# Moving a statistics pool ahead of the weight tiles in a fused attention and two-layer kernel

## The chip, the cores and the metric

The kernel runs on one core of one Trainium2 chip. The metric is the device time of one execution in microseconds (us). Before the change three executions took 976.26, 979.25 and 979.58 us; the median is 979.25 us.

## The reference, cut to what matters

Attention with rotary positions (4 batches, 8 heads, 576 positions, head size 64) gives x of 2304 tokens by 512. Two feed-forward layers follow, both in float32:

```python
# layer 1, weights 512x1536, 512x1536, 1536x512
gate = 1.0 / (1.0 + np.exp(-(x @ w_gate)))
val = x @ w_val
y = gate * val @ w_out
# layer 2, weights 512x1024 and 1024x512
h = y @ w_in
sm = softmax(h)                       # over the 1024 columns
solu = h * sm
ln = (solu - mean(solu)) / np.sqrt(var(solu) + 1e-06) * g_ln
out = ln @ w_out2
```

The weights arrive as 64-bit floats and are decoded on the core.

## The kernel before, in words

Every product is made of three matmuls: both factors are split into a high part and a low part (float32r), and high by high, high by low and low by high are added in PSUM. Below, the *stationary* operand of a matmul is the one loaded into the array (128 columns, 512 bytes per partition), the *moving* one is streamed through it (512 columns are 2048 bytes per partition).

**Attention (to about 320 us of the span).** 16 pairs of heads are worked off in 144 groups. The order of the work is written out by hand in slots (SLOTS and the agenda). A pair's sums of weights go through `weigh_out` (L398): they are transposed, copied into the small tile `rt` (VectorE, L401) and stored by a DMA in SyncE's queue (L403), once per pair, about 17.5 us apart. The stacked operands of the scores are brought together by five DMAs from SBUF to SBUF (`stack`, L306 to L314).

**Layer 1 (about 303 to 760 us).** 60 items: three sets of four feature tiles, each over five token blocks of 512, 512, 512, 256 and 512 columns. An item is `gate_val` (24 matmuls, L672 to L674: stationary is the weight tile `w`, moving the split activations `xs`) and, one item later, `out_part` (12 matmuls, L781 to L783: stationary `w`, moving `gs`). Between them ScalarE, VectorE and GpSimd make `gs` (L762 to L767). While an item runs, `make` decodes the next weights in one to two units per item (`w_decode`: L119 to L136 on ScalarE, VectorE and GpSimd), and `split_x` splits the next activations (L504 to L507). Weight tile number i lies in ring slot i modulo 6: slot 0 is the pool `wA`, slots 1 to 5 are the pool `wB`.

**Layer 2 (about 760 us to the end).** Weight units lie in the same ring, tiles 12 to 17, three units each; units 0 to 2 are in slot 0 (`wA`). For each of 18 token tiles, `hidden` runs 24 matmuls (L874 to L876: stationary the split tokens `ysp`, moving the weight units 0 to 7, so the first nine of them read `wA` and the other fifteen `wB`), `normalise` makes the statistics in a small tile `st`, and `project` runs 24 matmuls (L969 to L971: stationary the transposed tokens `lt`, moving the weight units 8 to 15).

**Where tiles lie.** Pools opened on the left side follow one another in the order in which they are opened, tiles padded to 32 bytes per partition; pools on the right side are laid from the upper end. What matters below is each tile's start address modulo 512 bytes, worked out from that order and the tile sizes:

| tile | role | start modulo 512 |
|---|---|---|
| `w` in `wA` | stationary in layer 1, moving in layer 2 | 192 |
| `w` in `wB` | stationary in layer 1, moving in layer 2 | 288 |
| `xs`, `gs` (right side) | moving in layer 1 | 480 |
| `ysp` (tiles 0 to 3, in `xs` buffers) | stationary in layer 2 | 480 |
| `ysp` (tiles 4 to 17, left side) | stationary in layer 2 | 288 |
| `lt` (right side) | stationary in layer 2 | 480 |
| `ident`, `qtl` (before all) | attention | 128, 192 |
| `e`, alternating buffers | attention, stationary in transposes | 160, 416 |
| `et`, `vs` | attention, moving and stationary | 160, 160 |
| `st` of scores, by tile | attention, both | 288 and 32 |

All steps inside a tile (high to low part, one 128-row piece to the next) are whole multiples of 512 bytes for the tiles of both layers, so the table gives the residue of every matmul operand of the layers. The pool `s2` (three tiles `st` of 32 bytes) is opened after `wA` and `wraw`.

```python
    wA = ctx.enter_context(tc.tile_pool(name="wA", bufs=1))
    wraw = ctx.enter_context(tc.tile_pool(name="wraw", bufs=2))
    s2_p = ctx.enter_context(tc.tile_pool(name="s2", bufs=3))
```

Of the kernel before, what the change touches and what calls it, by code (L numbers as in the profile page):

```python
# [8 lines left out]
F32 = mybir.dt.float32  # L9
# [11 lines left out]
def kernel(  # L21
# [26 lines left out]
    P = 128  # L48
# [5 lines left out]
    NS = 3  # L54

    const = ctx.enter_context(tc.tile_pool(name="const", bufs=1))
    wA = ctx.enter_context(tc.tile_pool(name="wA", bufs=1))
    wraw = ctx.enter_context(tc.tile_pool(name="wraw", bufs=2))
    s2_p = ctx.enter_context(tc.tile_pool(name="s2", bufs=3))
    wdec = ctx.enter_context(tc.tile_pool(name="wdec", bufs=2))  # L60

    ident = const.tile([P, P], F32, name="ident")
# [112 lines left out]
    enter = a_ctx.enter_context  # L175
# [3 lines left out]
    rot_p = prep_ctx.enter_context(tc.tile_pool(name="rot", bufs=1, side="right"))  # L179
    qk_p = enter(tc.tile_pool(name="qkT", bufs=2))  # L180
    wt_p = enter(tc.tile_pool(name="wt", bufs=2))
    uw_p = enter(tc.tile_pool(name="uw", bufs=4))
    st_p = enter(tc.tile_pool(name="st", bufs=4))
    et_p = enter(tc.tile_pool(name="et", bufs=1))
# [158 lines left out]
    NTL = len(order)  # L343
# [53 lines left out]

    def weigh_out(i):  # L398
        ps = wts[i]
        rt = wt_p.tile([NTL, P], F32, tag="rt", name=f"rt{i}")  # L400
        nc.vector.tensor_copy(rt, ps[:NTL, :P])  # L401
        d = dr_p.tile([NTL * P], F32, tag="d", name=f"d{i}")
        nc.sync.dma_start(out=d.rearrange("(n p) -> n p", p=P), in_=rt)  # L403
        wts[i] = d
# [180 lines left out]
    for i in range(NPR):  # L585
# [14 lines left out]
        for name, fn in (  # L600
            ("weigh", weigh), ("weigh_t", weigh_t), ("weigh_out", weigh_out), ("spread", spread), ("scale", scale_x)
        ):
            at(g + own[name], REST, fn, i)
# [75 lines left out]
    if True:  # L679
# [32 lines left out]
        for g in range(NPR * NTL):  # L712
            i, n = divmod(g, NTL)
# [83 lines left out]
    def split_y(t):  # L797
        if t < 4:
            s = xs_pool["p"].tile([P, 2, 512], F32R, tag="xs", name=f"ysp{t}")
            s = s.rearrange("p a (k t) -> p a k t", k=KD)  # L800
        else:
            s = ys_p.tile([P, 2, KD, P], F32R, tag="ys", name=f"ysp{t}")
        src = y_sb[:, :, t * P:(t + 1) * P]
        nc.scalar.copy(out=s[:, 0], in_=src)
        nc.gpsimd.tensor_sub(out=s[:, 1], in0=src, in1=s[:, 0].bitcast(F32))
        ysp[t] = s
# [28 lines left out]
    for t, (s, bl, f) in enumerate(items):  # L835
# [17 lines left out]
        if f % FG in (1, 2) and t + FG < len(items):  # L853
            s2, bl2, _ = items[t + FG]
# [4 lines left out]
    enter = c_ctx.enter_context  # L859
# [6 lines left out]
    def hidden(t, half):  # L866
        s = ysp[t]
        if half == 0:
            phs[t] = ps_2.tile([P, 2, 512], F32, tag="s", name=f"ph{t}")
        ph = phs[t]  # L870
        for kk in range(2 * half, 2 * half + 2):
            for n in range(2):
                wh, wl = unit(2 * kk + n)
                nc.tensor.matmul(ph[:, n, :], s[:, 0, kk, :], wh, start=kk == 0, stop=False)  # L874
                nc.tensor.matmul(ph[:, n, :], s[:, 0, kk, :], wl, start=False, stop=False)  # L875
                nc.tensor.matmul(ph[:, n, :], s[:, 1, kk, :], wh, start=False, stop=kk == KD - 1)  # L876

    def spare(name):
        return xs_pool["p"].tile([P, 2, 512], F32R, tag="xs", name=name).rearrange("p n c -> p (n c)").bitcast(F32)

    def normalise(t):

        ph = phs.pop(t)
        st = s2_p.tile([P, 8], F32, tag="st", name=f"st{t}")
        nm, sm, tsum, var, r, rv = (st[:, j:j + 1] for j in range(6))
        yield nc.vector.tensor_reduce(out=nm, in_=ph, axis=AX.XY, op=ALU.max, negate=True)
        if t == 0:
            e = spare("e2_0")
        else:
            e = h_p.tile([P, DF2], F32, tag="e", name=f"e2_{t}")  # L890
        ev = e.rearrange("p (n c) -> p n c", n=2)
        yield nc.scalar.activation(out=ev, in_=ph, func=AF.Exp, bias=nm, accum_out=sm)
        yield nc.vector.scalar_tensor_tensor(
            out=ev, in0=ph, scalar=1.0, in1=ev, op0=ALU.mult, op1=ALU.mult, accum_out=tsum
        )

        nc.vector.tensor_scalar_mul(tsum, tsum, -1.0 / DF2)
        nc.vector.tensor_scalar_add(r, sm, 1e-9)
        nc.vector.reciprocal(r, r)
        if t == 0:  # L900
            junk = spare("junk0")
        else:
            junk = j_p.tile([P, DF2], F32, tag="junk", name=f"junk{t}")
        yield nc.scalar.activation(out=junk, in_=e, func=AF.Square, bias=tsum, accum_out=var)
        nc.vector.tensor_scalar(out=rv, in0=var, scalar1=r, scalar2=r, op0=ALU.mult, op1=ALU.mult)
        nc.vector.tensor_scalar(out=rv, in0=rv, scalar1=1.0 / DF2, scalar2=1e-6, op0=ALU.mult, op1=ALU.add)
        nc.gpsimd.tensor_tensor(out=rv, in0=rv, in1=mhalf, op=ALU.pow)
        yield
        nc.vector.tensor_mul(out=rv, in0=rv, in1=r)
        nc.vector.tensor_scalar(out=e, in0=e, scalar1=tsum, scalar2=rv, op0=ALU.add, op1=ALU.mult)  # L910
        ln[t] = e
        yield
# [6 lines left out]
    def pack(t):  # L919

        upper, lower = halves(ln.pop(t))
        pk = pk_p.tile([P, 2, DF2], U16, tag="pk", name=f"pk{t}")
        copy(PACK[0], pk[:, 0], upper)
        copy(PACK[1], pk[:, 1], lower)
        tps[t] = tp_p.tile([P, 2 * KF, P], U16, tag="tp", name=f"tp{t}")
        nc.sync.dma_start_transpose(out=tps[t], in_=pk.rearrange("p a c -> p (a c)"))

    def unpack(t):

        tp = tps.pop(t).rearrange("p (a k) t -> p a (k t)", a=2)  # L930
        z = z_p.tile([P, DF2], F32, tag="z", name=f"z{t}")
        upper, lower = halves(z)
        copy(UNPACK[0], upper, tp[:, 0])
        yield copy(UNPACK[1], lower, tp[:, 1])
        lt = lts[t] = lt_p.tile([P, 2, KF, P], F32R, tag="lt", name=f"lt{t}")
        z = z.rearrange("p (k t) -> p k t", k=KF)
        yield nc.scalar.copy(out=lt[:, 0], in_=z)
        yield nc.vector.tensor_sub(out=lt[:, 1], in0=z, in1=lt[:, 0].bitcast(F32))
# [23 lines left out]
    def project(t, half):  # L962
        lt = lts[t]
        if half == 0:
            pos[t] = ps_o.tile([P, DM], F32, tag="o", name=f"po{t}")
        po = pos[t]
        for f in range(KF // 2 * half, KF // 2 * half + KF // 2):
            wh, wl = unit(8 + f)
            nc.tensor.matmul(po, lt[:, 0, f, :], wh, start=f == 0, stop=False)  # L969
            nc.tensor.matmul(po, lt[:, 0, f, :], wl, start=False, stop=False)  # L970
            nc.tensor.matmul(po, lt[:, 1, f, :], wh, start=False, stop=f == KF - 1)  # L971
        if half == 0:
            return
        ob = o_p.tile([P, DM], F32, tag="ob", name=f"ob{t}")
        nc.scalar.copy(out=ob, in_=po)

        c = t * P
        while c < (t + 1) * P:
            b, j = divmod(c, S)
            if j < MAIN:  # L980
                r, p = divmod(j, P)
                n = min(P - p, (t + 1) * P - c)
                dst = out[b * S:b * S + MAIN, :].rearrange("(p r) d -> r p d", r=4)[r, p:p + n, :]
            else:
                n = min(S - j, (t + 1) * P - c)
                dst = out[b * S + j:b * S + j + n, :]
            nc.sync.dma_start(out=dst, in_=ob[c - t * P:c - t * P + n, :])
            c += n
# [20 lines left out]
    def do(kind, t):  # L1009
        if kind == "H":  # L1010
            hidden(t, 0)
            hidden(t, 1)
            norms[t] = normalise(t)
        elif kind == "n":
            next(norms[t])
        elif kind == "u":
            if t not in unpacks:
                unpacks[t] = unpack(t)
            next(unpacks[t])
        elif kind == "Y":  # L1020
            split_y(t)
        elif kind == "P":
            pack(t)
        elif kind == "J":
            project(t, 0)
            if t == NTT - 2:
                turn_ln(NTT - 1)
            project(t, 1)
        elif kind == "M":
            for _ in make_steps(1):  # L1030
                pass
        elif kind == "C":
            x = written.pop(0)
            next(x)
            next(x)
        elif kind == "O":
            out_part(*items[-1])
        elif kind == "S":
            store_y(*items[-1])
        elif kind == "X":  # L1040
            open_pools()
        elif kind == "T":

            st = s2_p.tile([P, 8], F32, tag="st", name="table_in")
            nc.scalar.activation(out=st[:, 0:1], in_=mhalf, func=AF.Exp)


# [68 lines left out]
```

## Time and profile before

| what | value |
|---|---|
| profiled execution, its own time | 976.1 us |
| its span | 974.1 us |
| work outside the span | 2.0 us |
| TensorE busy | 935.9 us (96%) |
| VectorE, ScalarE, GpSimd busy | 648.6, 500.6, 444.8 us |
| granted TensorE clock, mean | 0.992 |

PE is TensorE's matmuls, PEld its weight loads, DVE VectorE, ACT ScalarE, POOL GpSimd, SPq the queue of SyncE. The end of a matmul in the records is modelled: one matmul of 512 columns shows 0.39 us although the next one starts 0.23 us after it. So a pace is read from the starts of neighbouring matmuls and not from their durations.

### The profile page before, as it was taken

The numbers are of one execution on the slowest core, as the hardware profiler recorded it, in microseconds if no ns is written. First come the engines' busy times: TensorE is split into PE (matmuls) and PEld (weight loads), VectorE is DVE, ScalarE is ACT, GpSimd is POOL, SyncE is SP. The second block draws the span as 40 slices with busy tenths as digits, with TensorE's granted clock in tenths as the row PEclk, the third lists the DMA queues.
The fourth block names the chain that finished last, engine by engine and source line by source line (L and its number), as shares of the span: only waits on it lengthen the run. The fifth ranks groups of instructions, "written<-read, shape, count | busy, mean of one in ns | idle before, by whom it ended". The sixth has DMA issues, their size and how long they took to land.

```text
span 974.1 us, 14436 instructions
## 1 busy us (share of the span) xinstructions
PE 935.9 (96%) x5128; PEld 801.7 (82%) x5128; DVE 648.6 (67%) x1073; ACT 500.6 (51%) x994; POOL 444.8 (46%) x356
## 2 busy tenths in 40 slices
PE   4999999999999899999999999999999989999998
PEld 3899889898898688898788898788898868888886
DVE  8999889899988945346245355445456787666561
ACT  4888889798986422133111123112123576666662
POOL 5668888879846533334413344324343531121110
PEclk9999999999999999999999999999999999999999
DMA  4666676576654220103001012100112334234231
GB/s 109 143 170 165 161 178 171 140 196 158 159 144 136 87 65 22 43 23 108 22 22 44 23 44 87 44 22 22 44 45 64 109 65 87 66 77 86 65 76 43
DMA packets 92311, 86.10 MB, mean 88 GB/s; under 512 B 52608, under 2 KB 77456, under 8 KB 92240
## 3 DMA queue, kind: packets, MB, share of 16 engines
q1 hardware_dynamic: 92240, 85.19, 34.7%
q8 instruction: 40, 0.66, 0.3%
q14 instruction: 31, 0.25, 0.1%
HBM read 46.83 MB, written 4.79 MB: 53 GB/s over the span
## 4 chain that ended last, share of the span: by engine, by line
PE 64%; DVE 13%; DMA 10%; POOL 5%; issue 3%; ACT 3%; SPq 2%; DVEq 0%; POOLq 0%; ACTq 0%
DMA st<-st 9%; PE gv L673 9%; PE gv L674 9%; PE gv L672 9%; PE y L783 4%; PE y L781 4%; PE y L782 4%; PE po L970 3%; PE po L969 3%; PE po L971 3%; PE ph L874 3%; PE ph L875 3%; PE ph L876 3%; DVE nm L371 3%; PE av L476 2%
## 5 line engine op out<-in xcount | busy, mean ns | idle before, releaser
L767 POOL TENSOR_TENSOR gs<-g,gs 128x512 fp32r<-128x512 f32 (+1 forms) x59 | 74.0, 1254 | 268.3 <-DVE gs L766 242.2
L762 ACT ACTIVATE sg<-gv 128x512 f32<-128x512 f32 (+1 forms) x60 | 33.3, 555 | 297.0 <-PE gv L674 297.0
L672 PE MATMUL gv<-xs,w 128*128 128x512 f32 (+1 forms) x480 | 179.1, 373 | 1.6 <-ACT w L135 1.6
L674 PE MATMUL gv<-xs,w 128*128 128x512 f32 (+1 forms) x480 | 179.1, 373 | 1.1 <-POOL w L136 1.1
L673 PE MATMUL gv<-xs,w 128*128 128x512 f32 (+1 forms) x480 | 179.1, 373 | 0.3 <-DVE xs L507 0.2
L764 DVE TENSOR_TENSOR g<-gv,sg 128x512 f32<-128x512 f32 (+1 forms) x60 | 38.2, 636 | 181.5 <-ACT sg L762 181.4
L364 PE MATMUL s<-st 128*128 128x288 f32 x512 | 103.9, 322 | 14.9 <-DMA st<-st 8.3
L376 ACT ACTIVATE e<-s,nm 128x576 f32<-128x576 f32 x144 | 107.3, 745 | 17.6 <-DVE nm L371 17.1
L371 DVE TENSOR_REDUCE nm<-s 128x1 f32<-128x576 f32 x144 | 107.2, 745 | 6.3 <-PE s L364 4.8
L672 PEld LDWEIGHTS gv<-xs,w 128*128 128x128 f32 x480 | 90.4, 188 | 19.4 <-ACT w L135 2.1
L674 PEld LDWEIGHTS gv<-xs,w 128*128 128x128 f32 x480 | 90.4, 188 | 19.3 <-POOL w L136 1.9
L673 PEld LDWEIGHTS gv<-xs,w 128*128 128x128 f32 x480 | 90.5, 189 | 19.1 <-DVE xs L507 1.9
L429 DVE TENSOR_TENSOR et<-te,et 128x512 fp32r<-128x512 f32 x144 | 98.3, 685 | 9.8 <-ACT et L426 8.4
L476 PE MATMUL av<-et,vs 128*128 128x288 f32 x512 | 100.9, 318 | 0.4 <-DVE uw L625 0.3
L364 PEld LDWEIGHTS s<-st 128*128 128x128 f32 x512 | 76.0, 195 | 24.8 <-ACT e L376 7.4
L783 PE MATMUL y<-gs,w 128*128 128x512 f32 (+1 forms) x240 | 89.2, 372 | 0.0
L781 PE MATMUL y<-gs,w 128*128 128x512 f32 (+1 forms) x240 | 89.1, 371 | 0.0
L782 PE MATMUL y<-gs,w 128*128 128x512 f32 (+1 forms) x240 | 89.1, 371 | 0.0
L426 ACT CAST et<-te 128x512 fp32r<-128x512 f32 x144 | 84.0, 585 | 7.1 <-PE te L435 7.0
L435 PE MATMUL te<-ident,e 128*128 128x128 f32 x576 | 87.2, 275 | 0.0
L476 PEld LDWEIGHTS av<-et,vs 128*128 128x128 f32 x512 | 74.1, 192 | 1.6 <-DVE uw L625 1.0
L435 PEld LDWEIGHTS te<-ident,e 128*128 128x128 f32 x576 | 71.5, 142 | 0.2
(128 smaller groups left out, 1960.6 us busy)
## 6 DMA issues: line engine op xcount, KB each, us to landing
wraw<-in_moe_w_out_dram SPq DMA_DIRECT2D x20, 512.0 KB, 3.8
st<-st SPq DMA_DIRECT2D x30, 288.0 KB, 3.1
st<-st SPq DMA_DIRECT2D x15, 432.0 KB, 4.0
wraw<-in_moe_w_gate_dram SPq DMA_DIRECT2D x12, 512.0 KB, 4.0
wraw<-in_moe_w_val_dram SPq DMA_DIRECT2D x12, 512.0 KB, 4.2
um<-uw SPq DMA_DIRECT2D x32, 144.0 KB, 2.5
st<-st SPq DMA_DIRECT2D x30, 144.0 KB, 4.9
rawv<-in_v_dram SPq DMA_DIRECT2D x16, 256.0 KB
```

Source lines behind the costliest of these rows:

```text
L364: nc.tensor.matmul(ps[:, j, :HALF], w, x, start=m == 0, stop=m == len(mm) - 1)
L371: nc.vector.tensor_reduce(out=nm, in_=ps[:, :, :HALF], axis=AX.XY, op=ALU.max, negate=True)
L376: nc.scalar.activation(out=e.rearrange("p (j c) -> p j c", j=2), in_=ps[:, :, :HALF], func=AF.Exp, bias=nm, accum_out=sums[i][:, sum_at[n] ...
L429: nc.vector.tensor_sub(out=l_out, in0=ps, in1=h_out.bitcast(F32))
L435: nc.tensor.transpose(ps[:, r * P:(r + 1) * P], e[:, r * P:(r + 1) * P], ident)
L476: nc.tensor.matmul(av[:, :HALF], *mm[m], start=m == 0, stop=m == len(mm) - 1)
L672: nc.tensor.matmul(ps[:, :n], wh, x[:, 0, :n], start=kk == 0, stop=False)
L673: nc.tensor.matmul(ps[:, :n], wh, x[:, 1, :n], start=False, stop=False)
L674: nc.tensor.matmul(ps[:, :n], wl, x[:, 0, :n], start=False, stop=kk == KD - 1)
L781: nc.tensor.matmul(ys[m][:, :n], wh, g[:, 0, :n], start=first, stop=False)
L782: nc.tensor.matmul(ys[m][:, :n], wl, g[:, 0, :n], start=False, stop=False)
L783: nc.tensor.matmul(ys[m][:, :n], wh, g[:, 1, :n], start=False, stop=last)
```

## The change

The pool `s2` is opened ahead of `wA`, and its tiles grow from 8 to 24 columns (32 to 96 bytes per partition, three tiles). No more than six columns are used, as before. The small tile `rt` leaves the pool `wt` (two buffers) for a pool of its own with one buffer, opened right after `wt`. No instruction is added or removed by the text of the change, and no order is changed.

By the same arithmetic as above, 288 bytes of `s2` now lie ahead of `wA`: `wA` starts at 480 modulo 512, and so do `wraw`, the decode tiles, `wB`, `y_sb` and `ysp` on the left side (all 192 bytes later than before). `xs`, `gs` and `lt` on the right side stay at 480. In attention the tiles behind `rt` move by 192 - 512 = -320 bytes, which modulo 512 is the same shift of 192; `ident`, `qtl` and the right side stay.

```diff
     const = ctx.enter_context(tc.tile_pool(name="const", bufs=1))
+
+
+    s2_p = ctx.enter_context(tc.tile_pool(name="s2", bufs=3))
     wA = ctx.enter_context(tc.tile_pool(name="wA", bufs=1))
     wraw = ctx.enter_context(tc.tile_pool(name="wraw", bufs=2))
-    s2_p = ctx.enter_context(tc.tile_pool(name="s2", bufs=3))
...
     wt_p = enter(tc.tile_pool(name="wt", bufs=2))
+    rt_p = enter(tc.tile_pool(name="rt", bufs=1))
...
-        rt = wt_p.tile([NTL, P], F32, tag="rt", name=f"rt{i}")
+        rt = rt_p.tile([NTL, P], F32, tag="rt", name=f"rt{i}")
...
-        st = s2_p.tile([P, 8], F32, tag="st", name=f"st{t}")
+        st = s2_p.tile([P, 24], F32, tag="st", name=f"st{t}")
...
-            st = s2_p.tile([P, 8], F32, tag="st", name="table_in")
+            st = s2_p.tile([P, 24], F32, tag="st", name="table_in")
```

## Rows read from the trace of the kernel before

**Rows 1.** The page: busy time by engine, slices of the span, chain by engine.
```profile
PE 935.9 (96%) x5128; PEld 801.7 (82%) x5128; DVE 648.6 (67%) x1073; ACT 500.6 (51%) x994; POOL 444.8 (46%) x356
PE   4999999999999899999999999999999989999998
PEclk9999999999999999999999999999999999999999
PE 64%; DVE 13%; DMA 10%; POOL 5%; issue 3%; ACT 3%; SPq 2%; DVEq 0%; POOLq 0%; ACTq 0%
```

**Rows 2.** Windows: stretch, length, busy us and count by engine, granted clock, DMA.
```profile
0.00:320.00 320.00, 292.69 (x2154) 274.70 (x2155) 289.68 (x488) 265.49 (x626) 238.06 (x189) 0.99 0.63 156
328.00:441.20 113.20, 112.97 (x557) 93.52 (x556) 58.19 (x83) 31.33 (x59) 41.31 (x32) 1.00 0.15 47
441.20:463.30 22.10, 21.91 (x95) 17.24 (x93) 13.72 (x22) 8.31 (x14) 10.70 (x9) 1.00 0.33 97
463.30:591.00 127.70, 127.67 (x620) 105.49 (x621) 57.23 (x90) 23.05 (x43) 43.51 (x34) 1.00 0.09 29
591.00:617.00 26.00, 25.96 (x111) 20.42 (x110) 16.45 (x24) 8.95 (x15) 13.14 (x10) 1.00 0.39 121
617.00:737.00 120.00, 120.00 (x588) 99.75 (x587) 53.16 (x83) 19.73 (x38) 39.84 (x32) 1.00 0.08 27
737.00:788.50 51.50, 48.24 (x206) 38.72 (x205) 41.17 (x61) 27.81 (x44) 25.26 (x19) 0.97 0.29 87
788.50:961.50 173.00, 173.00 (x760) 141.90 (x759) 110.14 (x218) 110.86 (x148) 29.52 (x31) 1.00 0.37 75
```

**Rows 3.** Timeline of PE, layer 1: start us, duration us, line, operands.
```profile
477.44 0.40 PE L672 MATMUL gv<-xs,w 128*128 128x512 f32 x1
...
483.05 0.39 PE L781 MATMUL y<-gs,w 128*128 128x512 f32 x1
...
640.14 0.40 PE L673 MATMUL gv<-xs,w 128*128 128x512 f32 x1
...
645.51 0.39 PE L672 MATMUL gv<-xs,w 128*128 128x512 f32 x1
```

**Rows 4.** Timeline of PE, layer 2, two token tiles.
```profile
830.93 0.39 PE L969 MATMUL po<-w,lt 128*128 128x512 f32 x1
...
836.42 0.40 PE L874 MATMUL ph<-w,ysp 128*128 128x512 f32 x1
...
838.52 0.39 PE L874 MATMUL ph<-w,ysp 128*128 128x512 f32 x1
...
841.93 0.39 PE L969 MATMUL po<-w,lt 128*128 128x512 f32 x1
```

**Rows 5.** Timeline of PE, layer 1, block of 256 columns.
```profile
410.15 0.28 PE L672 MATMUL gv<-xs,w 128*128 128x256 f32 x1
...
412.27 0.28 PE L672 MATMUL gv<-xs,w 128*128 128x256 f32 x1
...
415.77 0.28 PE L672 MATMUL gv<-xs,w 128*128 128x256 f32 x1
...
417.81 0.28 PE L672 MATMUL gv<-xs,w 128*128 128x256 f32 x1
```

**Rows 6.** Timeline of VectorE, three rounds of decoding ahead of item 40.
```profile
592.79 0.69 DVE L764 TENSOR_TENSOR g<-gv,sg 128x512 f32<-128x512 f32 x1 [0.68 <-ACT sg L762]
...
602.78 0.68 DVE L764 TENSOR_TENSOR g<-gv,sg 128x512 f32<-128x512 f32 x1
...
612.74 0.68 DVE L764 TENSOR_TENSOR g<-gv,sg 128x512 f32<-128x512 f32 x1
```

**Rows 7.** Waits in 612 to 618 and in 783 to 789 us: us, times, longest.
```profile
PEld gv L673 <- DVE xs L507: 0.8, 2, 0.5
...
PE ph L874 <- DVE e L893: 3.3, 1, 3.3
```

**Rows 8.** Timeline of PE in attention: two groups of transposes and what follows.
```profile
207.56 0.60 PE L435 MATMUL te<-ident,e 128*128 128x128 f32 x4
207.91 1.30 PE L476 MATMUL av<-et,vs 128*128 128x288 f32 x8
...
209.72 0.60 PE L435 MATMUL te<-ident,e 128*128 128x128 f32 x4
210.08 0.51 PE L476 MATMUL av<-et,vs 128*128 128x288 f32 x2
```

**Rows 9.** Chain that ended last: the stacking DMAs of neighbouring pairs (start, us).
```profile
58.98 4.89 DMA st<-st
64.48 3.31 DMA st<-st
...
76.14 4.96 DMA st<-st
81.67 3.55 DMA st<-st
```

**Rows 10.** Line 401, the copy into rt: count, duration, first and last start.
```profile
L401 DVE COPY rt<-tr x16: 268/269/271, 45.1 to 310.7; 9x128 f32<-9x128 f32 x16
```

## Prediction

> **What bounds the kernel now.** I read the page's busy times first: TensorE is busy 96% of the span, and nine tenths or more in nearly every slice [rows 1]. A busy share alone would not say that its pace is the limit, because matmul ends are modelled, so I cut the span into stretches. From 0 to 320 us four engines are busy 74 to 91% and none rules alone; the chain of waits there goes through VectorE, TensorE and DMAs. From 328 us on there are four long stretches in which TensorE is busy throughout (112.97 of 113.20, 127.67 of 127.70, 120.00 of 120.00, 173.00 of 173.00 us) and no other engine over 64% [rows 2]. In these, matmuls start back to back, and the time is the number of matmuls times their pace. Between them lie three short stretches, 441 to 463, 591 to 617 and 737 to 788 us, where decoding of the next weights sets the end: rounds of decoding take 9.99 and 9.96 us [rows 6], an item's 36 matmuls 36 x 0.2333 = 8.4 us, so the slack runs out and TensorE then waits: 0.8 us behind VectorE's split of `xs` at 615 us, 3.3 us behind `normalise` at 785 us [rows 7].
>
> The reader's question is thus the pace of one matmul, read from starts. In layer 1, 24 matmuls take 483.05 - 477.44 = 5.61 us with weights in `wA` (233.8 ns each), and 23 take 645.51 - 640.14 = 5.37 us with weights in `wB` (233.5 ns) [rows 3]. Layer 2 runs the same shape with other start addresses, side by side: `project` 24 in 5.49 us (228.8 ns), the first nine of `hidden`, whose moving weights lie in `wA`, 2.10 us (233.3 ns), the other fifteen, in `wB`, 3.41 us (227.3 ns, the first of them still slow; the rest start 226 or 227 ns apart) [rows 4]. The granted clock is 1.00 in all these stretches [rows 2], its higher level of 2.4 GHz, so the clock doesn't make the difference.
>
> **The change part by part.** *Addresses of both layers.* Take the difference, moving start less stationary start, modulo 512 bytes. Layer 1 has 480-288 = 192 (`wB`) and 480-192 = 288 (`wA`): 233.5 and 233.8 ns. `project` has 288-480 = 320: 228.8 ns. `hidden` has 192-288 = 416 for `wA`: 233.3 ns, and 288-288 = 0 for `wB`: 226.7 ns. The last two alternate within one token tile, with the same stationary tile, the same neighbours on the other engines and the same clock; only the address of the moving tile differs. That is the whole ground of this forecast: at difference 0 a matmul of 512 columns costs 226.7 ns, at the differences of layer 1 233.3 ns. The change puts every operand at 480, so difference 0 everywhere. For layer 1 the gain per matmul lies between 0 (the pace has another cause there) and 6.6 ns; I take 6.6, from the nearest row, or 2.83% of 233.3.
>
> For 256 columns `wA` takes 2.12 us for 18 (117.8 ns) and `wB` 2.04 us (113.3 ns) [rows 5]. 113.3 is half of 226.7, so I take it as the floor: 4.5 ns for `wA`, nothing for `wB`. The other end would be a loss of the same 4.5 ns for `wB`, 360 matmuls, 1.6 us.
>
> Now the sum, by stretches [rows 2]. A 256-column block is 144 matmuls, 16.6 us, of which 36 in `wA`.
> - 328 to 441: (113.2 - 16.6) x 2.83% + 36 x 4.5 ns = 2.9 us.
> - 463 to 591: (127.7 - 16.6) x 2.83% + 0.16 = 3.3 us.
> - 617 to 737: (120.0 - 16.0) x 2.83% = 2.9 us.
> - 788 to the end: a token tile takes 2.10 + 3.41 + 5.49 = 11.00 us [rows 4] and would take 48 x 226.7 = 10.88; 173 / 11.0 = 15.7 tiles, 1.9 us.
>
> Together 11.0 us. In the three short stretches I count nothing: there the end is set by decoding, whose instructions are the same, and a faster TensorE only waits longer for it. What is late next is thus `xs` at 463 and 615 us and `normalise` at 785 us. Without that cover (if decoding had room) they would give (22.1 + 26.0) x 2.83% + 1.2 = 2.6 us more, and the start of layer 1, where weights are also late, 0.5 us.
>
> *The bigger, earlier `st`.* Same instructions on the same six columns; only the distance between tiles grows. Nothing.
>
> *One `rt` buffer.* The copy L401 must now wait for the store of the pair before instead of the one two before. The copies run from 45.1 to 310.7 us, 16 of them, 17.7 us apart [rows 10]; the nearest DMA rows land within 5 us [rows 9]. The store is long done. Were it not, VectorE's row maxima and evacuations would queue behind L401, and the scores behind these: at most 15 x 5 us, at least nothing. I take nothing.
>
> *Attention's tiles.* All left tiles move by the same 192 modulo 512, so scores and weighted sums keep their differences; only `ident` and `qtl` don't move along. Transposes with `e` at 160 and at 416 both start the next kind of matmul 0.35 and 0.36 us after the first of four [rows 8], so they don't feel the address. Bounds: 6.6 ns on some 860 transposes and 128 `qtl` matmuls is 6.5 us either way if all lay on the path; I take 0. The stacking DMAs write rows that start at 288 in one pair and at 32 in the next (second tile), and the chain shows 4.89 and 3.31 us against 4.96 and 3.55 [rows 9]: no address effect to speak of, so the move to 480 and 224 costs nothing.
>
> The sum against the profiled execution: 976.1 - 11.0 = 965.1 us. The median of the runs, 979.25, is 3.2 us above that execution; with the same gain it gives 968.3. One run of three lies at the profiled one's level and two above, so I predict the middle, 966.7 us.
>
> *A rule against it.* "TensorE: Matmul & The Clock Gate" in the Trainium skill, section "Step-by-step: what each phase is for", says that TensorE reads SBUF through "two independent read ports", one for the moving and one for the stationary operand. By that rule where the two operands lie can't matter and the change would give 0, 976.1 us. The trace disagrees on `hidden`, 233.3 against 227.3 ns with nothing but an address different [rows 4]. The same page, section "Wait — 56ns, not 53.3ns?", has 215.7 ns between matmuls of 512 columns; no stretch here comes nearer than 226.7, so something beyond the column count is paid in every matmul of this kernel.
>
> **The rivals.**
> - *Nothing moves* (0.08): the pace of layer 1 has another cause, and layer 2's `wA` third is slow for being in another place, not for its difference. 976.1 us. For it: layer 1 has never been seen at difference 0. Against it: five differences fit one rule, and 233.3 appears in layer 2 as well, without layer 1's work around it.
> - *Only layer 2 gains* (0.06): GpSimd's and VectorE's work in layer 1 holds the pace at 233. 976.1 - 1.9 = 974.2 us. Against it: 617 to 737 and 328 to 441 have different loads on GpSimd and ScalarE [rows 2], and the pace doesn't differ.
> - *Decoding gives way too* (0.07): a faster TensorE frees ring slots and PSUM earlier and decoding moves up whole. 965.1 - 3.1 = 962.0 us.
> - *Attention pays* (0.04): the stacking copies, two steps on the chain in each of about ten pairs, depend on the start within 512 bytes, and at 480 and 224 the shorter step takes as long as the longer: 10 x (4.96 - 3.31) = 16.5 us, 965.1 + 16.5 = 981.6, slower than before. It decides from 1.1 us per pair on, where the gain is gone. Against it: the two starts of today cost the same.
>
> **How the numbers follow.** The forecast has the remaining 0.75. The range is 960 to 975 us: the lower end takes in 962.0 with a little of attention's bound, the upper one the layer-2 case and a part of the 256-column loss; beyond lie the no-change and the slower case. A measurement here tells about 0.5% (4.9 us) from no change. Faster by more: the forecast and the decoding case, 0.82. Within: nothing moves and layer 2 alone, 0.14. Slower: attention pays, 0.04.
>
> **What would show it.** Right: the starts of L672 to L674 and L781 to L783 226 to 227 ns apart, `project` and `hidden` all at 226 to 227, 256 columns at 113.3; `gv` waiting longer for `xs` near items 20 and 40 and `ph` longer near item 60; 0 to 320 us unchanged within 3 us. Wrong: layer 1 still at 233 with `hidden`'s first nine at 227 (then place counts otherwise than by difference), or a first 320 us longer by more than 5 us (then `rt`, `ident` or the DMAs pay).

## The result and the profile after

The changed kernel takes 966.43 us (median of 6, 964.68 to 971.62), the kernel before beside it 977.75 us (median of 6, 974.09 to 980.84). The ratio is 0.9913 with a 95% interval of 0.9888 to 0.9938: 0.6 to 1.1% faster. (The two medians lie 11.3 us apart; the middle of the ratio stands for 8.5 us.) The profiled execution took 966.59 us, its span 964.8 us.

The page of the changed kernel, lines that answer to [rows 1]:

```profile
PE 921.8 (96%) x5128; PEld 800.1 (83%) x5128; DVE 647.6 (67%) x1073; ACT 501.5 (52%) x994; POOL 443.5 (46%) x356
PE   4989989999999899999999999999999989999998
PEclk9999999999999999999999999999999999999999
PE 61%; DVE 14%; DMA 11%; POOL 5%; issue 5%; ACT 2%; SPq 2%; POOLq 0%; DVEq 0%; ACTq 0%
```

TensorE's busy time falls by 14.1 us while its number of instructions and the other engines' busy times stay within 1.3 us. The span falls by 9.3 us.

The windows of the changed kernel, cut at the same matmuls as [rows 2], the first 320 us excepted (stretch, length, busy us and count by engine, granted clock, DMA):

```profile
0.00:320.00 320.00, 290.14 (x2156) 272.01 (x2156) 289.72 (x488) 266.46 (x626) 237.32 (x189) 1.00 0.64 156
327.55:439.41 111.86, 111.29 (x558) 94.44 (x556) 58.27 (x84) 31.57 (x60) 41.34 (x32) 1.00 0.15 48
439.41:461.48 22.07, 21.58 (x96) 17.57 (x95) 14.05 (x22) 8.42 (x14) 11.01 (x9) 1.00 0.34 101
461.48:586.86 125.38, 125.34 (x621) 106.37 (x620) 56.72 (x90) 23.10 (x43) 43.21 (x34) 1.00 0.09 29
586.86:612.66 25.80, 25.29 (x110) 20.30 (x109) 16.63 (x24) 9.03 (x15) 13.15 (x10) 1.00 0.37 123
612.66:730.74 118.08, 118.08 (x589) 100.64 (x588) 53.29 (x83) 19.90 (x38) 39.75 (x32) 1.00 0.08 27
730.74:780.77 50.03, 46.26 (x206) 37.74 (x204) 39.88 (x59) 26.82 (x43) 25.09 (x19) 1.00 0.24 84
780.77:952.34 171.57, 171.22 (x759) 141.46 (x758) 110.58 (x220) 111.32 (x150) 29.42 (x31) 1.00 0.38 77
```

From starts of the same matmuls in both traces, the difference (after less before) by stretch:

| stretch of before, us | forecast | measured |
|---|---|---|
| 0 to 302 (attention) | 0 | -1.4 |
| 302 to 328 (start of layer 1) | 0 | +1.0 |
| 328 to 441 | -2.9 | -1.3 |
| 441 to 464 (decoding) | 0 | -0.3 |
| 464 to 591 | -3.3 | -2.2 |
| 591 to 617 (decoding) | 0 | -0.1 |
| 617 to 737 | -2.9 | -2.0 |
| 737 to 789 (decoding) | 0 | -1.6 |
| 789 to 969 | -1.9 | -1.3 |
| sum | -11.0 | -9.2 |

Of the 9.2 us, 6.8 went where they were forecast to go, in four stretches, and each gave less than forecast. The paces say why. Timeline of PE in the changed kernel: the same matmuls as [rows 3], then as [rows 4] without the split at `wB`, then as [rows 5] (start us, duration us, line, operands):

```profile
475.00 0.39 PE L675 MATMUL gv<-xs,w 128*128 128x512 f32 x1
...
480.44 0.39 PE L784 MATMUL y<-gs,w 128*128 128x512 f32 x1
...
635.13 0.39 PE L676 MATMUL gv<-xs,w 128*128 128x512 f32 x1
...
640.34 0.39 PE L675 MATMUL gv<-xs,w 128*128 128x512 f32 x1
...
823.16 0.39 PE L972 MATMUL po<-w,lt 128*128 128x512 f32 x1
...
828.60 0.39 PE L877 MATMUL ph<-w,ysp 128*128 128x512 f32 x1
...
834.04 0.39 PE L972 MATMUL po<-w,lt 128*128 128x512 f32 x1
...
407.92 0.28 PE L675 MATMUL gv<-xs,w 128*128 128x256 f32 x1
...
410.07 0.28 PE L675 MATMUL gv<-xs,w 128*128 128x256 f32 x1
...
413.54 0.28 PE L675 MATMUL gv<-xs,w 128*128 128x256 f32 x1
...
415.69 0.28 PE L675 MATMUL gv<-xs,w 128*128 128x256 f32 x1
```

512 columns: 5.44 us for 24 with `wA`, 5.21 for 23 with `wB`, 5.44 for 24 in `project` and in `hidden`: 226.5 to 226.7 ns in all of them. 256 columns: 18 take 2.160 us by the unrounded starts, 120.0 ns with `wA` (117.8 before) and with `wB` (113.3 before). These became slower.

Waits of the changed kernel in 608 to 614 and in 776 to 782 us, answering to [rows 7] (us, times, longest):

```profile
PEld gv L676 <- DVE xs L510: 1.4, 2, 0.9
...
PE gv L676 <- DVE xs L510: 0.5, 1, 0.5
...
PE ph L877 <- DVE e L896: 3.3, 1, 3.3
```

The weight load behind `xs` waited 0.8 us and now waits 1.4: TensorE works its items off faster, and the decoding behind which it waits takes as long as before.

### The profile page after: what moved, and what is told of

Its sections match the earlier page's. It is cut to its first block, busy times and chain, and to the rows that moved or that the text cites. A ratio compares the mean times of both kernels' runs of the same rounds, so it can differ in the third digit from the quotient of the medians.

```text
span 964.8 us, 14429 instructions
## 1 busy us (share of the span) xinstructions
PE 921.8 (96%) x5128; PEld 800.1 (83%) x5128; DVE 647.6 (67%) x1073; ACT 501.5 (52%) x994; POOL 443.5 (46%) x356
## 4 chain that ended last, share of the span: by engine, by line
PE 61%; DVE 14%; DMA 11%; POOL 5%; issue 5%; ACT 2%; SPq 2%; POOLq 0%; DVEq 0%; ACTq 0%
PE gv L676 9%; PE gv L677 9%; DMA st<-st 9%; PE gv L675 9%; PE y L786 4%; PE y L785 4%; PE y L784 4%; PE po L974 3%; PE po L973 3%; PE po L972 3%; PE ph L878 2%; PE ph L877 2%; PE ph L879 2%; DVE nm L374 2%; DVE val L123 2%
## 5 line engine op out<-in xcount | busy, mean ns | idle before, releaser
L767 DVE TENSOR_TENSOR g<-gv,sg 128x512 f32<-128x512 f32 (+1 forms) x60 | 38.2, 637 | 175.6 <-ACT sg L765 175.6
```

## Experiments

Theory: the pace of these matmuls hangs on the difference of the start addresses of moving and stationary operand. Rivals: the single `rt` buffer or the moved tiles of attention; the start at 480 itself or `s2` ahead of the weights; a fixed cost of something else. Each experiment was timed beside the kernel before.

### rt_alone: the rt part by itself

```diff
+    rt_p = enter(tc.tile_pool(name="rt", bufs=1))
...
-        rt = wt_p.tile([NTL, P], F32, tag="rt", name=f"rt{i}")
+        rt = rt_p.tile([NTL, P], F32, tag="rt", name=f"rt{i}")
```

> The kernel before with only the single buffer for rt, so that attention's tiles behind it move by 512 bytes, which leaves every start modulo 512 as it was. Theory: layer 1 stays at 233.3 ns a matmul of 512 columns and the time stays at 977 us, within 0.3%. Rival (a part of the gain is attention's, by the one buffer or the tiles' places): 974 us or less, with the first matmul of layer 1 about 1.5 us earlier.

975.41 us against 974.99, ratio 1.0002 (0.9983 to 1.0022). Layer 1 stays at 233 ns: in its timeline 23 matmuls take 5.36 us.

```profile
643.00 0.39 PE L674 MATMUL gv<-xs,w 128*128 128x512 f32 x1
...
648.36 0.40 PE L673 MATMUL gv<-xs,w 128*128 128x512 f32 x1
```

Its first layer-1 matmul came 3.4 us later than in the profile before, that of the other variants 0.7 to 3.6 us earlier, wrong_amount among them, which isn't faster: attention differs by that much between executions, so the 1.4 us of the table above aren't counted for the change.

### right_shift: the difference closed from the other side

```diff
+    gap_p = ctx.enter_context(tc.tile_pool(name="gap", bufs=1, side="right"))
+    gap = gap_p.tile([P, 48], F32, name="gap")
+    nc.vector.memset(gap, 0.0)
     x_ctx = ExitStack()
```

on the kernel before, with the `rt` part for room.

> The kernel before, left side of weights as it was, with the single rt buffer for room and 192 idle bytes at the upper end, so that xs, gs, lt start at 288 instead of 480. Stationary and moving then meet at difference 0 for the weights in wB (both 288), and at 96 for those in wA. Theory (difference counts): layer 1 in wB 226.7 ns for 512 columns and 120.0 for 256, project 226.7, wA at 96 unknown, time about 968 us (five sixths of the gain of layer 1). Rival (the start at 480 counts, or s2 ahead of the weights): layer 1 stays at 233.3 and the time at 977 us.

968.20 us against 974.99, ratio 0.9942 (0.9920 to 0.9963). Timeline of PE, `wB` of 512 columns first, then `wA`, then `project`, then 256 columns in `wB`:

```profile
634.35 0.39 PE L677 MATMUL gv<-xs,w 128*128 128x512 f32 x1
...
639.56 0.39 PE L676 MATMUL gv<-xs,w 128*128 128x512 f32 x1
...
473.27 0.39 PE L676 MATMUL gv<-xs,w 128*128 128x512 f32 x1
...
478.87 0.40 PE L785 MATMUL y<-gs,w 128*128 128x512 f32 x1
...
823.28 0.39 PE L973 MATMUL po<-w,lt 128*128 128x512 f32 x1
...
828.73 0.40 PE L878 MATMUL ph<-w,ysp 128*128 128x512 f32 x1
...
411.69 0.28 PE L676 MATMUL gv<-xs,w 128*128 128x256 f32 x1
...
413.85 0.28 PE L676 MATMUL gv<-xs,w 128*128 128x256 f32 x1
```

`wB`, at difference 0, takes 5.21 us for 23 (226.5 ns); `wA`, at 96, 5.60 for 24 (233.3); `project` 5.45 for 24 (227); 256 columns 2.16 for 18 (120.0). The pace follows the difference, at 288 as at 480, with `s2` where it was.

### wrong_amount: the whole change with another width

```diff
-        st = s2_p.tile([P, 24], F32, tag="st", name=f"st{t}")
+        st = s2_p.tile([P, 16], F32, tag="st", name=f"st{t}")
```

on the changed kernel (and the same in `table_in`).

> The changed kernel with st of 16 columns instead of 24: s2 stands ahead of the weights as in the change and rt has its one buffer, but the left side moves by 96 bytes instead of 192, so w is at 384 and xs, gs, lt at 480. Differences: layer 1 96, project 416, hidden 0 for both wA and wB (left ysp at 384). Theory (difference alone, paces from the address probe): 512 columns of layer 1 233.7 ns, 256 columns 120.0, project 233.9, hidden 226.7 to 228: against the kernel before 0.5 + 2.6 + 2.1 - 0.9 = 4.3 us more, about 979 us. Rival (s2 ahead of the weights, wider st or the order of the pools gains, whatever the amount): 966 us.

977.16 us against 975.11, ratio 1.0028 (1.0012 to 1.0044): slower than the kernel before by 1.2 to 4.3 us, with 4.3 expected. Timeline of PE, layer 1, then `project`, `hidden` in `wA` and in `wB`, then 256 columns:

```profile
638.00 0.39 PE L676 MATMUL gv<-xs,w 128*128 128x512 f32 x1
...
643.36 0.40 PE L675 MATMUL gv<-xs,w 128*128 128x512 f32 x1
...
830.16 0.39 PE L972 MATMUL po<-w,lt 128*128 128x512 f32 x1
...
835.77 0.39 PE L877 MATMUL ph<-w,ysp 128*128 128x512 f32 x1
...
837.84 0.39 PE L877 MATMUL ph<-w,ysp 128*128 128x512 f32 x1
...
841.24 0.39 PE L972 MATMUL po<-w,lt 128*128 128x512 f32 x1
...
412.37 0.28 PE L675 MATMUL gv<-xs,w 128*128 128x256 f32 x1
...
414.53 0.28 PE L675 MATMUL gv<-xs,w 128*128 128x256 f32 x1
```

5.36 us for 23 (233.0 ns), `project` 5.61 for 24 (233.8, it was 228.8 before), `hidden` 2.07 for 9 and 3.40 for 15 (230 and 227), 256 columns 120.0. Every part of the change is there but the amount, and the gain is gone.

### probe_address: the dependence by itself

Its loops, shortened:

```python
    for n in (512, 256, 384, 288):
        for d in range(0, 128, 4):        # float32 columns: steps of 16 bytes
            group(k, n, d, 0)             # 24 matmuls: columns, moving start, stationary start
    for s in range(0, 128, 16): group(k, 512, s, s)
    for s in range(0, 128, 16): group(k, 512, (s + 48) % 128, s)
```

> Leaves out the whole computation: only streams of 24 matmuls, float32r, one stream for each start difference (moving less stationary) of 0, 16, 32 ... 496 bytes, for 512, 256, 384 and 288 columns; then 512 columns with both operands moved together by 0, 64 ... 448 bytes at difference 0, and the same at difference 192. Theory (the pace hangs on the difference alone): 512 columns 226.7 ns at difference 0, 233 at 192, 288 and 416, 229 at 320; 256 columns 120.0 at 0, 113.3 at 192, 117.8 at 288; moving both together changes nothing. Rival (the place of a tile counts, not the difference): one pace at all differences of a column count, or other values in the two last series.

Mean pace in ns, worked out from the starts of the last 20 matmuls of each stream (256 to 496 bytes repeat 0 to 240 within 1.7 ns, nearly all within 0.3; the first stream, partly at 1.2 GHz, is replaced by the first of the next series):

| columns | 0 | 16 | 32 | 64 | 96 | 112 | 128 | 160 | 192 | 224 | 240 |
|---|---|---|---|---|---|---|---|---|---|---|---|
| 512 | 226.7 | 231.7 | 233.2 | 229.2 | 233.7 | 231.4 | 232.3 | 233.8 | 233.3 | 233.3 | 226.7 |
| 384 | 173.3 | 175.6 | 173.3 | 173.1 | 176.7 | 173.2 | 176.0 | 173.3 | 176.7 | 173.3 | 179.8 |
| 288 | 131.7 | 130.0 | 133.3 | 132.1 | 131.7 | 134.7 | 133.3 | 133.2 | 133.3 | 133.0 | 131.7 |
| 256 | 119.6 | 118.7 | 116.7 | 118.0 | 120.0 | 113.3 | 118.4 | 117.3 | 113.3 | 118.5 | 117.2 |

Windows over the last two series, difference 0 and then 192, with the common start going through all residues:

```profile
516.00:558.00 42.00, 42.00 (x185) 34.53 (x184) 0.00 (x0) 0.00 (x0) 0.00 (x0) 1.00 0.00 0
560.00:602.00 42.00, 42.00 (x182) 33.72 (x181) 0.00 (x0) 0.59 (x1) 0.00 (x0) 1.00 0.30 113
```

Three matmuls more in 42 us at difference 0 (226.7 to 228.2 ns by starts; the 228.2 take in some ten slower matmuls after each entry, then all streams run at 226.7) than at 192 (233.3 in all eight streams): the common start doesn't matter. Two things stand against the theory as it was put: the period is 256 bytes, not 512, and which difference is best changes with the number of columns. 0 is the best one for 512 and among the worst for 256.

### block_shift and block_112: another difference for the 256-column block

```diff
+SHIFT = {512: 0, 256: 48}
...
-            nc.tensor.matmul(ps[:, :n], wh, x[:, 0, :n], start=kk == 0, stop=False)
+            nc.tensor.matmul(ps[:, :n], wh, x[:, 0, cols(n)], start=kk == 0, stop=False)
```

on the changed kernel (in block_112 28 stands for 48), `cols(n)` being columns SHIFT[n] to SHIFT[n] + n, and alike wherever `xs` and `gs` are written or read.

> The changed kernel, in which the block of 256 columns uses columns 48 to 303 of its tiles xs and gs, so that its difference is 192 again while that of 512 columns stays 0. Theory: 256 columns take 113.3 ns instead of 120.0, 432 matmuls, 2.9 us less than the changed kernel (966.4 to 963.5 us), nothing else moves. Rival (the 120 ns come from the neighbours' placement, not from the difference): 120.0 ns stays, 966.4 us.

> The changed kernel with the block of 256 columns at columns 28 to 283 of its tiles, difference 112, while 512 columns stay at 0. Theory: 113.3 ns for 256 columns as in the address probe, 432 x 6.7 = 2.9 us less than the changed kernel, about 963.5 us. Rival (a stream of 256 columns keeps one of several paces, set by how it is entered, as the 117.8 ns at difference 192 hint): 118 to 120 ns, 965.5 us or more.

after_again is the changed kernel beside block_112:

> The changed kernel once more, beside the next ones on the same chip. Theory and rivals alike: 966 us, 512 columns at 226.7 ns, 256 columns at 120.0 ns in every block.

after_again 965.88 us, ratio 0.9921 (0.9892 to 0.9950), 120.0 ns in every 256-column stream. block_shift 964.40, 0.9891 (0.9875 to 0.9907); block_112 964.83, 0.9895 (0.9874 to 0.9915). Their medians are 1.0 to 1.5 us below after_again's, and by the ratios the distance is 2.5 to 2.9 us, but the intervals overlap, so the timing alone doesn't set them apart from the changed kernel. Timeline of PE, 18 matmuls in block_shift, then in block_112:

```profile
412.31 0.28 PE L683 MATMUL gv<-xs,w 128*128 128x256 f32 x1
...
414.43 0.28 PE L683 MATMUL gv<-xs,w 128*128 128x256 f32 x1
```

```profile
412.49 0.28 PE L683 MATMUL gv<-xs,w 128*128 128x256 f32 x1
...
414.56 0.28 PE L683 MATMUL gv<-xs,w 128*128 128x256 f32 x1
```

2.12 us (117.8 ns) at difference 192, in every stream, where the kernel before had 113.3 at that same difference; 2.07 (115.0) at 112, where the last matmuls of the stream run at 113.3, and 113.3 in most of its other streams. So the forecast of block_shift failed: 2.2 ns a matmul were gained instead of 6.7. In block_112 the pace came out nearly as forecast: by the starts, the stretches 328 to 441, 464 to 591 and 617 to 737 us take 2.4 us less than in after_again's profile, with 2.9 expected.

The stretch of the wait behind `normalise` has to be kept apart from this. It takes 51.67 us at a granted clock of 0.95 in block_112 and 50.03 at 1.00 in the profile of the changed kernel above. But after_again, which is the changed kernel itself, has 51.64 at 0.95 there, so the 1.6 us are a difference between executions. The same matmuls in block_112, then in after_again:

```profile
727.33:779.00 51.67, 47.86 (x205) 38.93 (x204) 41.23 (x63) 27.73 (x44) 25.01 (x19) 0.95 0.29 88
```

```profile
731.02:782.66 51.64, 47.90 (x206) 38.95 (x205) 41.51 (x63) 27.73 (x44) 25.02 (x19) 0.95 0.30 88
```

### probe_entry: one pair of addresses, two paces

> Leaves out the whole computation: streams of 48 matmuls of 256 and of 512 columns at differences 0, 112, 192 and 240, each entered from 24 matmuls of five other kinds (512 columns at 0, 192 or 112, 256 at 112, 288 at 144). Theory (the difference alone sets the pace): one pace per column count and difference, whatever came before: 256 columns 120.0, 113.3, 113.3, 117.2; 512 columns 226.7, 231.4, 233.3, 226.7. Rival (the pace also hangs on how the stream is entered): 256 columns at 192 show 113.3 after some and 117.8 after others, and other pairs may split as well.

Pace in ns of the second half of 48 matmuls, by what ran before (columns at difference):

| stream | after 512 at 0 | 512 at 192 | 512 at 112 | 256 at 112 | 288 at 144 |
|---|---|---|---|---|---|
| 256 at 0 | 120.0 | 120.0 | 120.0 | 120.0 | 120.0 |
| 256 at 112 | 113.3 | 113.2 | 113.3 | 113.3 | 113.3 |
| 256 at 192 | 117.8 | 113.3 | 113.3 | 113.3 | 117.8 |
| 256 at 240 | 117.0 | 117.0 | 117.0 | 117.1 | 117.1 |
| 512 at 0 | 226.7 | 226.7 | 226.7 | 226.7 | 226.7 |
| 512 at 112 | 231.4 | 231.4 | 231.4 | 230.8 | 230.8 |
| 512 at 192 | 233.3 | 233.3 | 233.3 | 233.3 | 233.3 |
| 512 at 240 | 233.3 | 236.7 | 236.7 | 236.7 | 233.3 |

Entered from 512 columns at 0, as in block_shift, 256 at 192 runs at 117.8; entered from 512 at 192, as in the kernel before, at 113.3. The theory needs this addition: the difference fixes which paces there are, and at some differences the entry picks one, which then stays. The kind of stream ahead isn't all that picks it. 18 matmuls of the same instructions at the same start addresses modulo 512, after the same matmuls, third set of layer 1, in the kernel before and in rt_alone:

```profile
718.57 0.28 PE L672 MATMUL gv<-xs,w 128*128 128x256 f32 x1
...
720.61 0.28 PE L672 MATMUL gv<-xs,w 128*128 128x256 f32 x1
```

```profile
721.54 0.28 PE L673 MATMUL gv<-xs,w 128*128 128x256 f32 x1
...
723.66 0.28 PE L673 MATMUL gv<-xs,w 128*128 128x256 f32 x1
```

2.04 and 2.12 us (113.3 and 117.8 ns). What set these two apart stays open. Difference 0 has one pace for 512 columns after all five kinds of stream.

### probe_load: is it the weight load?

Its loops, shortened (a stream has 36 matmuls, not the 24 of the expectation):

```python
    for n in (512, 256):
        for c in (128, 64, 32):           # stationary columns
            for d in range(0, 64, 4):
                group(k, n, d, 0, 36, c)
```

> Leaves out the whole computation: streams of 24 matmuls, 512 and then 256 moving columns, with stationary tiles of 128, 64 and 32 columns, at differences 0, 16, 32 ... 240 bytes. Theory (the extra over one clock cycle per column comes from the weight load and the stream reading at the same time; at difference 0 it is 32 cycles of 2.4 GHz for a load of 512 bytes, 226.7 - 213.3 and 120.0 - 106.7 ns): with 64 stationary columns the extra at difference 0 halves to 6.7 ns (220.0 and 113.3 ns), with 32 columns it is 3.3 ns (216.7 and 110.0), and the spread over the differences shrinks in the same measure. Rival (a fixed cost of a matmul, or one of the moving stream alone): 226.7 and 120.0 ns at difference 0 whatever the stationary tile.

Windows over the 576 matmuls of 512 columns with 128, 64 and 32 stationary columns (second number in brackets: weight loads):

```profile
17.00:150.60 133.60, 133.60 (x578) 108.23 (x577) 0.00 (x0) 0.00 (x0) 0.00 (x0) 1.00 0.00 1
150.60:282.80 132.20, 132.20 (x578) 77.28 (x577) 0.00 (x0) 0.00 (x0) 0.00 (x0) 1.00 0.00 0
282.80:416.00 133.20, 133.20 (x578) 62.43 (x577) 0.00 (x0) 0.00 (x0) 0.00 (x0) 1.00 0.00 1
```

Weight loads are busy 108, 77 and 62 us, the streams take 133.6, 132.2 and 133.2. At difference 0 the pace is 226.7, 230.0 and 231.7 ns for 512 columns, where 220.0 and 216.7 were expected, and 120.0, 116.7 and 117.8 for 256. So neither the theory nor its rival holds: the pace at difference 0 doesn't fall in the measure of the load (for 512 columns it rises), and it isn't the same whatever the stationary tile. The lowest over all differences is 226.7 for each of the three loads, and 113.3 for 256 columns. So at the best difference the 13.3 and 6.7 ns over one cycle per column don't shrink with the load: 226.7 and 113.3 ns, 17/16 of a 2.4 GHz cycle per column, look like a floor of the moving stream at these two column counts. (In probe_address the lowest of 384 and of 288 columns are 173.1 and 130.0, above 17/16, which would be 170.0 and 127.5.) The 0 to 13 ns above the floor change with the start addresses, and a shorter load distributes them otherwise over the differences. Averaged over the differences they are 5, 3 and 5 ns for 512 columns; for 256 columns, whose 576 matmuls take 67.9, 67.2 and 66.2 us, they are 4.6, 3.3 and 1.7. So a shorter load takes a part away for 256 columns, and shows no trend for 512.

## Why the prediction was right, and where it was off

- **The bound.** Right: TensorE's pace ruled in four stretches, and these gave 6.8 of the 9.2 us in the table.
- **512 columns, 226.7 ns at difference 0.** Right, in nearly all streams of both layers, and right_shift, wrong_amount and probe_address show that the difference is the cause. It was read from two neighbouring rows in one token tile that differ in one address [rows 4].
- **256 columns.** The term that was mis-sized. I took 113.3 ns as a floor that `wB` keeps and `wA` reaches (0.3 us gained). Measured: 120.0 for all 432, 360 x 6.7 + 72 x 2.2 = 2.6 us lost, beyond the bound of 1.6 us that I gave. The error was to carry a rule for 512 columns over to 256, where the trace had two differences and neither was 0. 11.0 - 0.3 - 2.6 = 8.1 us is what the sum should have been, against 6.8 measured in the four stretches; of the remaining 1.3, by the starts, 0.6 are a new wait of TensorE at 802 us in layer 2 and 0.4 longer waits at 334 to 340 us. The wait at 802 us isn't in after_again's profile.
- **Cover by decoding.** Right for 441 to 464 and 591 to 617: 22.07 and 25.80 us against 22.40 and 25.86 from the same matmuls, the wait for `xs` longer. In 737 to 789 us 1.6 us went, but not because decoding moved up: before, the wait of 3.3 us behind `normalise` was followed by 3.4 us at 1.2 GHz, with matmuls 0.43 us apart (granted clock 0.97 in the stretch [rows 2]), in the changed kernel's profile not (1.00), in block_112 and in after_again, the changed kernel once more, again (0.95). That is a difference between executions and no gain of the change.
- **rt, attention, st.** Right: nothing came of them, for `rt` by rt_alone. For attention's tiles the result was right and the reason wasn't: `e` at 160 and at 416, and the stacked rows at 288 and at 32, lie 256 bytes apart, which is the period that probe_address shows for matmuls, so two equal times were no evidence that the address doesn't count. Evidence for it is that the transposes start 109 ns apart (median) before and after, though `e` has moved by 192 against `ident`. No run tests the stacking DMAs by themselves.
- **The time.** 966.7 predicted, 966.43 measured, and that the two agree to 0.3 us is luck. The forecast took 11.0 us off a start of 977.7, the middle of two readings. By the ratio the gain is 6.1 to 10.9 us of 977.75, middle 8.5, and 11.0 lies just above that interval. Beside the experiments the kernel before took 974.99 and 975.11 us (medians of 18 each). Measured by these and by the ratio, a start too high by some 2.7 us and a gain too high by some 2.5 cancelled.
- **The rule against it.** "TensorE: Matmul & The Clock Gate" in the Trainium skill ("Step-by-step: what each phase is for") says that TensorE has two independent read ports, from which I took it that addresses can't matter. The trace disagrees: 233.3 and 226.7 ns at 2.4 GHz in probe_address, at differences 192 and 0 with nothing else changed.

The lowest median of all is block_shift's (964.40 us); what it has over the changed kernel is shown by the pace, 117.8 for 120.0 ns, and not by the timing.

Open: what collides in the chip. That the difference of the two starts counts, and not their common start, suggests that the two reads meet somewhere; probe_load, where a shorter load helped at 256 columns and not at 512, doesn't tell where.

## What to carry to other kernels

Where TensorE runs back to back, work out its pace from the starts of neighbouring matmuls and compare it across stretches of one shape: a few per cent at full clock can be the start addresses of the two operands, and a pad changes them (192 bytes here). Try the difference for each column count that the kernel uses, since the best one for 512 columns was nearly the worst for 256. Expect less than pace times count: what decodes or normalises beside TensorE gets no faster and turns a part of the gain into a wait.

## What was not expected of the hardware

- The dependence repeats every 256 bytes: differences 96 and 352, for example, both give 233.7 ns (512 columns), 112 and 368 both 113.3 ns (256 columns).
- 256 columns at difference 0 take 120.0 ns, 13.3 over one cycle per column, the same 13.3 as 512 columns (226.7), while at 112 they take 113.3.
- At some differences a stream locks into one of two paces and keeps it: 113.3 or 117.8 ns for 256 columns at 192, 233.3 or 236.7 for 512 at 240, where the first probe, stepping there from its neighbour, even had 226.7.
